# Attention and a residual MLP on one core: twelve products moved from GpSimd to VectorE, one turn moved by a step, and a bias added on VectorE in place of 48 matmuls

## The chip, the core and the metric

The kernel runs on one core of one Trainium2 chip. Five engines work side by side, each in the order of its own queue: TensorE (PE; its weight loads are listed as PEld), VectorE (DVE), ScalarE (ACT), GpSimd (POOL) and SyncE (SP), which only issues DMAs. Semaphores tie the queues together. The metric is the device time of one execution in microseconds; the time of a kernel is the median over its runs.

## What is computed

Attention with 16 query heads and 4 key/value heads over 8 batches of 384 positions, and behind it a mixer: a product over tokens and a two-layer product over channels, each with an affine map ahead of it and a residual sum. In the reference:

```python
scores = scale * np.matmul(q, k.transpose(0, 1, 3, 2))
attn = exp(scores - max) / sum
x = np.matmul(attn, v)                    # to (8, 384, 1024)

a1 = alpha1 * x + beta1
tok = np.einsum('ts,bsd->btd', w_tok, a1)
u = x + lam * tok
a2 = alpha2 * u + beta2
ch = np.maximum(a2 @ w_ch1, 0.0) @ w_ch2  # 1024 -> 4096 -> 1024
return u + lam * ch
```

Inputs and output are float32; matmuls run in bf16 with float32 sums.

## The kernel before

**Pairs and products.** The batches are worked in four pairs. Each pair has a *first product* (with w_ch1, to 4096 channels) and a *second product* (with w_ch2, back to 1024), and both are written as seven products over blocks in place of eight; `o` (1 to 7) numbers them. `pair(i)` is a generator that yields between small portions of matmuls, called steps below. In the first pair it delegates to `first_product` (matmuls at L681) and `second_product` (L752); in the other three the matmuls stand at L831 and L897.

**The side work.** Attention, the token product and what feeds the next pair are done by `side(b)`, one call for each batch. While pair `i` is in its second product, the side work of batches 2i+2 and 2i+3 runs between its steps; batches 0 and 1 come ahead of everything. For each of eight column pieces `p` of 128 columns there are the scores (L260) with the exponential on ScalarE (L269), the product with v (`av`, L295), the division by the sum (L300 a reciprocal, L303), then a1, then the *token product* (`tok`, L324), on VectorE the residual sum (L331) and alpha2 (L334), and at last the *turn*: the piece is transposed so that the next pair can take it as an operand, by DMA (L337) or, for batches 0 and 3 and the last pieces of odd batches, by TensorE (`turn`, L398) with a copy on ScalarE (L400). Scores, `av`, token products and turns of batches 2 and up take their PSUM from three banks in rotation (`three()`).

**lam and alpha1, beta1.** lam is multiplied into alpha1 and beta1 once, so the token product comes out scaled. For batches 0 to 3 (`fold`) only alpha1 is applied on VectorE (L309), and beta1 enters in the token product: behind the nine matmuls of L324, three at a time, there stand three more (L328) that multiply two small matrices, R (row sums of w_tok) and H (lam x beta1). For batches 4 to 7 beta1 is added on VectorE: L312 writes alpha1 x to float32, L313 adds beta1 and writes bf16. The vector for this, `h1`, has lam x beta1 on all 128 partitions and shares its memory with R and H (`folded`). It is filled by `rows4_on` (two memsets on POOL, two row loads on SP), `to_all` (two shuffles on VectorE, L1037) and `scale_beta` (two products on VectorE, L1040); before the change they run in the second pair's first product.

**Results.** The second product leaves float32 blocks of 128x512 in `hT`. `scaled` multiplies each with lam (L790) and stores it with a DMA from POOL's queue that adds to the output (L442). `flush` runs one waiting `scaled` at certain steps. In the first pair the L790 stands on POOL, in the others on VectorE. In the next pair's first product ScalarE copies partial sums into the same memory (L836), so these copies wait for the stores' landing. In the last 12 steps of `second_product` six such results are flushed, and three more in the next pair's first product.

**Weights.** The w_ch1 chunks are loaded by DMAs on POOL's queue (L183); VectorE makes the block sums of them (L510, L515), for which it waits for the load. L448 to L450 and L850 on VectorE make block sums of the turned pieces. L499 and L603 on VectorE make block sums of w_ch2 and of the hidden values, L767 adds partial results of the second product, L764 and L744 on ScalarE copy such results out of PSUM and back. In the first product of the first pair L693 to L722 on VectorE evacuate PSUM and L561, L565 make block sums.

**Order.** All engines run in an order written by hand (`manual_schedule`): the order in which the program calls the operations is the order of each queue. `put(ps, phase, at, f, ...)` places a call at step `at` of pair `ps`, in its first (0) or second (1) product; `side(b)` gives its own table of steps (0 to 42), which is shifted by 38 for the second batch of a pair. So an operation placed a step later can fall behind another one on each queue that both use.

Of the kernel before, what the change touches and what calls it, by code (L numbers as in the profile page):

```python
# [13 lines left out]
def kernel(  # L14
# [21 lines left out]
    nc = tc.nc  # L36
# [4 lines left out]
    MUL = mybir.AluOpType.mult  # L41
# [43 lines left out]
    g1, h1, al2, lam_t = (vecs[:, i] for i in range(4))  # L85
# [10 lines left out]
    turn, a2_turn = [0], [0]  # L96
# [117 lines left out]
    def side(b):  # L214
        vb = vt[b % 2]
        ess, avs, a1s, a2s, xr = {}, {}, {}, {}, {}
        first, fold = b < 2, b < 4
        kT_, qT_ = kTs.get(b, kT), qTs.get(b, qT)

        def x_of(p):  # L220
# [170 lines left out]
        def by_pe(p):  # L391
            return b in (0, 3) or b % 2 and p >= NP - (4 if first else 3)
# [14 lines left out]
        def put(k, *m):  # L407
            at.setdefault(k, []).append(m)
# [3 lines left out]
        for p in range(NP):  # L412
            put((4, 10, 14, 18, 24, 29, 33, 35)[p], av, p)
            put((8, 15, 17, 22, 27, 32, 36, 38 if b % 2 else 39)[p], tok_flip, p)
            if by_pe(p):
                put(((13, 20, 22, 28, 34, 37, 40, 42) if b == 3 else (0, 0, 0, 0, 0, 36, 39, 41))[p], turn, p)
        return at

    def loads(b):
# [21 lines left out]
    def store(b, ms, dw, o):  # L441
        nc.gpsimd.dma_start(out=by_tok(out[b])[:, ms, dw * 512:(dw + 1) * 512], in_=o, accum_op=ADD)  # L442
# [19 lines left out]
    def spare(i):  # L462
        at = 24 * S + i % 3 * 1024
        return hTf[:, at:at + 1024]
# [102 lines left out]
    def free_blocks(side, gp):  # L567
        for kind in (side + "1", side + "2"):
            if (kind, gp) in block_slot:
                free(block_slot.pop((kind, gp)))  # L570
# [201 lines left out]
    def pair(i):  # L772
        b0 = 2 * i
        lead = i == 0
# [12 lines left out]

        def scaled(o, b, ms, dw, t):
            if o != 2 or not last:
                (nc.gpsimd if lead else nc.vector).tensor_tensor(out=t, in0=t, in1=lam_t[:, dw * 512:(dw + 1) * 512], op=MUL)  # L790
            store(b, ms, dw, t)

        def flush(n=9):
# [18 lines left out]
        if lead:  # L812
            yield from first_product(flush)
            share_banks("sc0", "acc", "sc1", "sc2")
            yield from second_product(pairs["acc"], later, flush, scaled)
            return

        for g in range(NH // 2):
            X, Y, snap = {}, {}, {}
            for k, (o, e) in enumerate(SEQ1):  # L820
                t = 2 * g + e
# [54 lines left out]
        for k, o in enumerate(PLACE2):  # L876
            whole = not last and o != 4
            tail = last and o == 4
            for h in range(1 if whole else 2):
                for ms in range(NST - (tail and not h)):  # L880
# [37 lines left out]
                    if (whole or h == 1) and not (last and o == 4):  # L918
                        if o in (1, 6, 5):
                            q = ((1, 6, 5).index(o) * NST + ms) * 512  # L920
                            snap[o, ms] = snaps[:, q:q + 512]
                        else:
                            bb, dw = where[o]
                            t = snap[1, ms] if o == 7 else spare(ms).bitcast(f32)
                        for c0, c1, x in X[ms]:
                            if o == 1:
                                nc.scalar.copy(out=snap[o, ms], in_=x)
                            elif o in (6, 5):
                                tt(out=snap[o, ms], in0=x, in1=snap[1 if last or o == 6 else 6, ms], op=ADD)
                            elif o == 2 and last:  # L930
                                tt(out=t, in0=x, in1=lam_t[:, :512], op=MUL)
                            else:
                                base = {2: 1, 3: 1 if last else 5, 7: 5, 4: 6}[o]
                                tt(out=t[:, c0:c1], in0=x, in1=snap[base, ms][:, c0:c1], op=ADD)
                            if o == 7 and not last:
                                tt(out=snap[6, ms], in0=x, in1=snap[6, ms], op=ADD)
                        if o not in (1, 6, 5):
                            later.append((scaled, o, b0 + bb, ms, dw, t))
# [8 lines left out]
    with tc.manual_schedule(engines=order):  # L947
# [123 lines left out]
        def put(ps, phase, at, *m):  # L1071
            plan.setdefault((ps, phase, at), []).append(m)
# [17 lines left out]
        put(0, 0, 8, rows4_on, (3, 0), (3, 1))  # L1090
        put(0, 0, 30, to_all, 3, 0, 0)
        put(0, 0, 34, to_all, 3, 1, 1)
        put(1, 0, 20, rows4_on, (1, 0), (1, 1))
        put(1, 0, 54, to_all, 1, 0, 0)
        put(1, 0, 68, to_all, 1, 1, 1)
        put(1, 0, 62, scale_beta, 0)
        put(1, 0, 76, scale_beta, 1)
        for c in range(4):
            put(0, 0, (50, 72, 74, 44)[c], load_w2, "11", c)
            put(0, 0, (6, 14, 42, 46)[c], cast_w2, "21", c)  # L1100
# [11 lines left out]
        for ps in range(NB - 1):  # L1112
            c = 2 * ps + 2
            for i in range(9):
                put(ps, 0, (4, 8, 12, 16, 20, 24, 54, 58, 62)[i] if ps == 0 else 4 + 7 * i, load_next, c, 1)
                put(ps, 0, 70 + 3 * i if ps == 0 else 91 + 2 * i, load_next, c + 1, 1)
            put_flips(ps, 0, c, (44, 46, 50, 54, 58) if ps == 0 else range(76, 86, 2))
            put_all(ps, 1, side(c))
            for u, f, h in zip((8, 14, 14, 27, 32, 33) if ps == 0 else (10, 17, 18, 28, 33, 33),
                               (flip_q, flip_k, flip_q, flip_q, flip_k, flip_q), (0, 0, 2, 4, 2, 6)):  # L1120
                put(ps, 1, u, f, c + 1, h, 2)
            put_all(ps, 1, side(c + 1), lambda u: u + 38)
            for j, u in ((0, 77), (2, 80), (3, 83)) if ps == 0 else ((0, 76), (2, 79), (3, 81)):
                put(ps, 1, u, sums_a, j, 1 if j else 2)

        def steps(ps):
            done = [0, 0]
            for second in pair(ps):
                for f, *a in plan.pop((ps, second, done[second]), []):
                    f(*a)  # L1130
                done[second] += 1
                yield
            for key in [k for k in plan if k[0] == ps]:
                for f, *a in plan.pop(key):
                    f(*a)

        first = steps(0)
# [76 lines left out]
```

## Time and profile before

| what | value |
|---|---|
| median of 3 runs | 732.6 us (731.02, 732.6, 734.45) |
| profiled execution, its own time | 731.92 us |
| its span in the trace | 729.9 us |
| TensorE clock granted | 1.00 throughout |
| first product of the first pair (L681), last part | up to 128 us |
| second product of the first pair (L752) | 128 to 234 us |
| first product of the second pair (L831) | 234 to 309 us |
| VectorE busy, 200 to 250 us | 42.8 of 50 us |
| TensorE busy, 200 to 250 us | 48.2 of 50 us |

Times in the trace count from the start of the span. A row such as "PE MATMUL C<-w,arena 128*128 128x512" gives engine, operation, what is written and read by the program's names, and the sizes. Neighbouring matmuls overlap, so what one costs is read from the distance of starts, not from the row's length. In brackets stands how long the engine had been idle and what it waited for. The engines' busy shares and the rows around the change are shown in the prediction.

### The profile page before, as it was taken

The numbers are of one execution on the slowest core, as the hardware profiler recorded it, in microseconds if no ns is written. First come the engines' busy times: TensorE is split into PE (matmuls) and PEld (weight loads), VectorE is DVE, ScalarE is ACT, GpSimd is POOL, SyncE is SP. The second block draws the span as 40 slices with busy tenths as digits, with TensorE's granted clock in tenths as the row PEclk, the third lists the DMA queues.
The fourth block names the chain that finished last, engine by engine and source line by source line (L and its number), as shares of the span: only waits on it lengthen the run. The fifth ranks groups of instructions, "written<-read, shape, count | busy, mean of one in ns | idle before, by whom it ended". The sixth has DMA issues, their size and how long they took to land.

```text
span 729.9 us, 14511 instructions
## 1 busy us (share of the span) xinstructions
PE 717.4 (98%) x5716; PEld 408.7 (56%) x5716; DVE 543.9 (75%) x1009; ACT 373.8 (51%) x566; POOL 199.2 (27%) x242
## 2 busy tenths in 40 slices
PE   8899999999999999999999999999999999999998
PEld 4665555555555666555555566655555566654444
DVE  7888876577888988649678888748868988763354
ACT  7877666544563666643433466663333366650000
POOL 8844233221046551201022344200002222000011
PEclk9999999999999999999999999999999999999999
DMA  9999999999999999969989999998989999937965
GB/s 164 180 239 231 190 195 227 226 242 235 366 312 232 179 182 196 234 221 207 272 193 220 160 162 194 212 227 201 270 233 183 210 126 146 165 123 264 302 174 104
DMA packets 197616, 153.26 MB, mean 210 GB/s; under 512 B 90540, under 2 KB 175892, under 8 KB 197292
## 3 DMA queue, kind: packets, MB, share of 16 engines
q0 software_dynamic: 109872, 64.47, 65.4%
q1 hardware_dynamic: 86988, 87.42, 42.8%
q8 instruction: 44, 0.72, 0.4%
q10 hardware_dynamic: 688, 0.46, 0.2%
q14 instruction: 24, 0.20, 0.1%
HBM read 155.23 MB, written 39.85 MB: 267 GB/s over the span
## 4 chain that ended last, share of the span: by engine, by line
PE 90%; DVE 4%; POOL 2%; DMA 1%; issue 1%; ACT 1%; DVEq 0%; ACTq 0%; POOLq 0%
PE C L897 30%; PE X L831 17%; PE C L752 10%; PE Y L831 9%; PE Z L831 4%; PE sc L260 4%; PE X L681 4%; PE sc L295 3%; PE sc L324 3%; PE Y L681 3%; DMA ops<-obuf 1%; DVE pad L565 1%; PE Z L681 1%; PE tok L324 1%; POOL obuf L334 0%
## 5 line engine op out<-in xcount | busy, mean ns | idle before, releaser
L897 PE MATMUL C<-w,arena 128*128 128x512 bf16 (+2 forms) x744 | 168.3, 372 | 0.0
L269 ACT ACTIVATE es<-sc 128x1024 bf16<-128x1024 f32 x108 | 104.1, 1024 | 116.0 <-PE sc L260 107.6
L897 PEld LDWEIGHTS <-arena 128*128 128x128 bf16 x1040 | 94.8, 98 | 100.5 <-issue 5.1
L442 POOL DMA_DIRECT2D out_dram<-hT x45 | 40.0, 888 | 294.7 <-DVE hT L790 135.9
L836 ACT ACTIVATE hT<-X,bias 128x384 f32<-128x384 f32 x144 | 83.6, 582 | 60.0 <-PE X L831 55.2
L831 PEld LDWEIGHTS <-w 128*128 128x128 bf16 x768 | 75.1, 98 | 50.0
L831 PEld LDWEIGHTS <-pad 128*128 128x128 bf16 x576 | 56.4, 98 | 37.2
L183 POOL DMA_DIRECT2D w<-in_moe_w_ch_dram x48 | 45.4, 1002 | 105.6 <-PE X L831 36.5
L831 PE MATMUL X<-ops,w 128*128 128x384 bf16 x384 | 70.3, 326 | 0.0
L831 PE MATMUL X<-ops,pad 128*128 128x384 bf16 x384 | 70.3, 326 | 0.0
L897 PE MATMUL C<-pad,arena 128*128 128x512 bf16 (+2 forms) x296 | 70.2, 373 | 0.0
L324 PEld LDWEIGHTS <-wtokT 128*128 128x128 bf16 x576 | 39.0, 98 | 16.4 <-issue 3.4
L752 PEld LDWEIGHTS <-arena 128*128 128x128 bf16 x336 | 29.8, 98 | 30.0 <-issue 2.5
L331 DVE TENSOR_TENSOR xr<-sc,xr 128x384 f32<-128x384 f32 x48 | 26.5, 553 | 25.6 <-PE sc L324 14.3
L752 PE MATMUL C<-w,arena 128*128 128x512 bf16 x168 | 41.2, 379 | 0.0
L838 DVE TENSOR_TENSOR arena<-Y,hT 128x384 bf16<-128x384 f32 x48 | 26.5, 556 | 17.7 <-ACT hT L836 16.0
L295 PEld LDWEIGHTS <-es 128*128 128x128 bf16 x864 | 32.8, 97 | 11.3
L831 PE MATMUL Y<-ops,w 128*128 128x384 bf16 x192 | 39.1, 326 | 0.0
L831 PE MATMUL Z<-ops,w 128*128 128x384 bf16 x192 | 39.0, 326 | 0.0
L269 ACT ACTIVATE hT<-sc 128x1024 bf16<-128x1024 f32 x36 | 35.8, 1031 | 4.3 <-PE sc L260 4.0
L260 PE MATMUL sc<-qT,kT 64*128 64x384 bf16 (+2 forms) x504 | 37.2, 271 | 0.5 <-ACT hT L269 0.2
L842 ACT ACTIVATE arena<-X,bias 128x384 bf16<-128x384 f32 x48 | 27.9, 582 | 17.7 <-PE X L831 16.1
(190 smaller groups left out, 1175.1 us busy)
## 6 DMA issues: line engine op xcount, KB each, us to landing
w<-w2s SPq DMA_DIRECT2D x67, 512.0 KB, 5.1
w<-in_moe_w_ch_dram POOLq DMA_DIRECT2D x65, 512.0 KB, 9.8
pad<-w2s SPq DMA_DIRECT2D x25, 512.0 KB, 6.9
out_dram<-hT POOLq DMA_DIRECT2D x45, 256.0 KB, 7.1
out_dram<-xr SPq DMA_DIRECT2D x48, 192.0 KB, 5.3
q_raw<-in_q_dram POOLq DMA_DIRECT2D x28, 192.0 KB, 9.5
w2s<-w SPq DMA_DIRECT2D x10, 512.0 KB, 7.6
arena<-in_moe_w_ch_dram POOLq DMA_DIRECT2D x8, 512.0 KB, 15.9
```

The source lines that it names most:

```text
L183: nc.gpsimd.dma_start(out=w1[:, w1_slots[c]], in_=w1src[:, :, c * CW * P:(c + 1) * CW * P])
L260: nc.tensor.matmul(out=sc[:, hh, k % 4:k % 4 + n], lhsT=kT_[r, 2 * p // G, BLK[hh][sk], :], rhs=qT_[r, p, st:st + n, :], start=True, stop= ...
L269: nc.scalar.activation(out=e, in_=sc, func=EXP, scale=scale_qk)
L295: nc.tensor.matmul(out=av[:, hh, sq, :], lhsT=ess[k // 4][:, m % 2, k % 4, :], rhs=vb[:, sk, hk, :], start=(sk == 0), stop=(sk == NST - 1))
L324: nc.tensor.matmul(out=ps[:, tt, :], lhsT=wtokT[:, st, tt * P:(tt + 1) * P], rhs=a1s[p][:, st, :], start=(st == 0), stop=(st == NST - 1 an ...
L442: nc.gpsimd.dma_start(out=by_tok(out[b])[:, ms, dw * 512:(dw + 1) * 512], in_=o, accum_op=ADD)
L681: nc.tensor.matmul(out=ps[:, :n], lhsT=tb[G, o][:, dt, e * P:(e + 1) * P], rhs=opb(FIRST1[o], n)[:, dt], start=(o in (1, 2, 7) and dt == 0 ...
L752: nc.tensor.matmul(out=x, lhsT=lead_hid[:, t, FIRST2[o], ms * P:(ms + 1) * P], rhs=rhs[:, t % 4 * 512:(t % 4 + 1) * 512], start=(o in (1, ...
L831: nc.tensor.matmul(out=ps, lhsT=tb[g, o][:, dt, e * P:(e + 1) * P], rhs=opb(LEFT1[o])[:, dt], start=(o in (1, 2, 7) and dt == 0), stop=(dt ...
L836: nc.scalar.activation(out=snap[o, e], in_=ps, func=IDENT, bias=hi if o == 5 else lo)
L842: nc.scalar.activation(out=hid[:, t, 4], in_=ps, func=RELU, bias=hi)
L897: nc.tensor.matmul(out=x, lhsT=hid[:, t, LEFT2[o], ms * P:(ms + 1) * P], rhs=rhs[:, t % 4 * 512 + c0:t % 4 * 512 + c1], start=((not last o ...
```

## The change

Four edits, in the order of the diff:

- `fold` now holds for batches 0 and 1 alone. Batches 2 and 3 lose the three L328 matmuls in each of their 16 token products (48 in all); L309 becomes L312 and L313.
- Batch 3's turn of piece 2 moves from step 22 to step 23 of its table. At step 22 stands also the token product of piece 3, which was called after the turn and is now called before it.
- `scaled` uses VectorE in the first pair too: 12 L790 leave POOL's queue for VectorE's (nine in the second product, three in the next pair's first product). Their stores stay on POOL's queue.
- `h1` is filled in the first product of the first pair: row loads at step 40, shuffles at steps 54 and 64, scalings at 59 and 69. They leave the second pair's first product.

```diff
     def side(b):
         vb = vt[b % 2]
         ess, avs, a1s, a2s, xr = {}, {}, {}, {}, {}
-        first, fold = b < 2, b < 4
+        first = fold = b < 2
...
             if by_pe(p):
-                put(((13, 20, 22, 28, 34, 37, 40, 42) if b == 3 else (0, 0, 0, 0, 0, 36, 39, 41))[p], turn, p)
+                put(((13, 20, 23, 28, 34, 37, 40, 42) if b == 3 else (0, 0, 0, 0, 0, 36, 39, 41))[p], turn, p)
...
         def scaled(o, b, ms, dw, t):
             if o != 2 or not last:
-                (nc.gpsimd if lead else nc.vector).tensor_tensor(out=t, in0=t, in1=lam_t[:, dw * 512:(dw + 1) * 512], op=MUL)
+                nc.vector.tensor_tensor(out=t, in0=t, in1=lam_t[:, dw * 512:(dw + 1) * 512], op=MUL)
             store(b, ms, dw, t)
...
-        put(1, 0, 20, rows4_on, (1, 0), (1, 1))
-        put(1, 0, 54, to_all, 1, 0, 0)
-        put(1, 0, 68, to_all, 1, 1, 1)
-        put(1, 0, 62, scale_beta, 0)
-        put(1, 0, 76, scale_beta, 1)
+        put(0, 0, 40, rows4_on, (1, 0), (1, 1))
+        for i in range(2):
+            put(0, 0, 54 + 10 * i, to_all, 1, i, i)
+            put(0, 0, 59 + 10 * i, scale_beta, i)
```

The order of VectorE's queue around the last token products of the first pair is, in the changed program (new rows marked with +; p counts batch 3's pieces):

```
L331 L334 (p5)  L767  L499
L300 L303 L312 +L313 (p6)  +L790
L300 L303 L312 +L313 (p7)  +L790
L331 L334 (p6)  +L790
L331 L334 (p7)  L515  L448 L449 L450  +L790
```

## The prediction

> **What bounds the kernel now.** I read the page's busy shares first, then who TensorE waited for, then every engine in order of time in the second product of the first pair (127 to 234 us) and in the start of the second pair, since the change lies there. The page:
>
> ```profile
> PE 717.4 (98%) x5716; PEld 408.7 (56%) x5716; DVE 543.9 (75%) x1009; ACT 373.8 (51%) x566; POOL 199.2 (27%) x242
> ```
>
> TensorE sets the end: of 729.9 us it is idle 12.5. So what is removed from its queue counts in full unless a wait takes its place. The waits of TensorE in the window 126 to 236 us (engine, line, waited for, us in total, times, longest):
>
> ```profile
> PE sc L324 <- DVE a L309: 0.9, 1, 0.9
> PE sc L324 <- ACT es L269: 0.6, 1, 0.6
> PE sc L398 <- ACT es L269: 0.2, 1, 0.2
> ```
>
> There are three, 1.8 us together. TensorE's rows in order of time (start, length, row) show both prices, one token product's matmuls and the longest of these waits:
>
> ```profile
> 217.85 0.33 PE L324 MATMUL sc<-a,wtokT 128*128 128x128 bf16 x3
> 218.02 0.22 PE L328 MATMUL sc<-vecs 128*128 128x128 bf16 x1
> 218.07 0.33 PE L324 MATMUL sc<-a,wtokT 128*128 128x128 bf16 x3
> ...
> 222.78 1.03 PE L752 MATMUL C<-w,arena 128*128 128x512 bf16 x4
> 224.76 0.34 PE L324 MATMUL sc<-a,wtokT 128*128 128x128 bf16 x3 [0.95 <-DVE a L309]
> ```
>
> From 217.85 to 218.07 four matmuls start, so one costs 0.056 us, though its row is 0.22 long (they overlap). The group at 222.78 takes 0.87 (next starts in unbroken stretches), so the row at 224.76 could have begun at 223.65: 1.11 us lost. VectorE was late because of these rows (VectorE in order of time; then the two forms of L790, min/median/max ns):
>
> ```profile
> 220.26 0.69 DVE L767 TENSOR_TENSOR hT<-C,hT 128x512 f32<-128x512 f32 x1 [0.39 <-ACT hT L764]
> 220.87 2.02 DVE L499 TENSOR_TENSOR w<-w,pad 128x2048 bf16<-128x2048 bf16 x1
> ...
> 223.62 1.08 DVE L309 TENSOR_TENSOR a<-xr,vecs 128x384 bf16<-128x384 f32 x1
> ```
> ```profile
> L790 DVE TENSOR_TENSOR hT<-hT,vecs x30: 679/684/693, 328.6 to 716.4; 128x512 f32<-128x512 f32 x30
> L790 POOL TENSOR_TENSOR hT<-hT,vecs x12: 1263/1559/2112, 142.8 to 263.6; 128x512 f32<-128x512 f32 x12
> ```
>
> L499 takes 1.22 elsewhere and L309 0.557: both are stretched exactly while POOL runs an L790.
>
> **The change, part by part.** *48 matmuls (L328) gone*: 48 x 0.0567 = 2.72 us, all on TensorE in the second product, whose rows abut there.
>
> A page differs: the Trainium skill, "TensorE: Matmul & The Clock Gate", section "Back-to-back issue gap", gives about 81 ns for a sustained 128-column matmul with its weight load, which would make 48 x 0.081 = 3.9 us and my sum 1.2 us lower. The trace's 0.056 contradicts it and decides.
>
> *The turn of piece 2 of batch 3 behind a token product.* The 0.59 us wait at 204.89 is a token product that wants a PSUM bank whose exponential ends at 204.80, because the turn at 203.97 took the bank before it. In the new order the product takes the bank that was free, and the turn, 0.5 + 0.87 later, the one freed at 204.80. I count -0.59 (bounds -0.59 and 0). The 0.2 wait stays (bounds -0.24 and 0).
>
> *Products with lam (12 x L790) to VectorE, and one addition more (16 x L313, 0.557 us).* VectorE gets 12 x 0.684 + 16 x 0.557 = 17.1 us more, 9 of the 12 in this product, and loses the stretching (L334 1.77 for 0.56, L499 2.02 for 1.22, two L309 1.08 and 1.74 for 0.56). What decides is where a token product waits. I lay VectorE's new order end to end from the end of batch 3's token product 5 (218.69), by start distances in the rows (L331 to L334 0.59, L334 0.48, L499 1.13, L300 0.23, L303 and L312 0.59, L767 and L790 0.60, last L313 0.56): L767 starts at 1.57 (it waits for ScalarE, as now), L499 2.18, L300 3.31, L303 3.54, L312 4.13, L313 4.72 to 5.28. Token product 6 could start at 4.96, so it waits about 0.38 where it waited 1.11: -0.73 (bounds -1.11 and +0.2). Product 7 waits 0.07 more. The earlier ones have 0.6 to 4 us between L309's end and the product, against 0.59 for the addition: nothing counted.
>
> *beta1's two shuffles and two scalings to the first product (90 to 110 us).* There VectorE idles 2.1 us in each group of 14 steps, which hides the work. But the first shuffle (0.62 of queue) stands before L702, which ends its first half at 101.13, and TensorE overwrites that bank at 101.40: 0.62 - 0.27 = 0.35 lost; the second scaling does it again one group on. +0.7 (bounds 0 and 4 x 0.65 = 2.6, all of it on the path). Where they leave, in the second pair, TensorE never waited: 0. The two memsets (0.6 each) on POOL and two row loads on SP go ahead of weight loads and flips with POOL idle 5.1 us at 77.9: 0, or 1.2 if a load is late.
>
> *The last product with lam, and who waits for it.* POOL took its six late L790 whenever data was there; VectorE takes them at their place in the order. POOL's rows, before:
>
> ```profile
> 225.19 1.56 POOL L790 TENSOR_TENSOR hT<-hT,vecs 128x512 f32<-128x512 f32 x1
> 227.05 0.87 POOL L442 DMA_DIRECT2D out_dram<-hT  x1 [0.30 <-POOL hT L790]
> 232.10 0.92 POOL L183 DMA_DIRECT2D w<-in_moe_w_ch_dram  x1 [4.17 <-PE sc L398]
> ```
>
> In the new order the sixth stands behind the additions L448 to L450. Going on with the same ledger: L790 5.20, L300 5.80, L303, L312, L313 to 7.77, L790 7.69, L331 and L334 8.29, L790 9.36, L331 and L334 9.96, L515 11.03, L448 to L450 11.64, last L790 13.17 to 13.85, its store 0.3 later: 14.16. Call T the end of token product 7, 228.17 before and 8.50 in the ledger. The last store went at T-1.1 and goes at T+5.7; the w1 load that stands behind it on POOL's queue went at T+3.9 and goes at T+6.6. Both are awaited early in the second pair:
>
> ```profile
> 237.23 1.18 ACT L836 ACTIVATE hT<-X,bias 128x384 f32<-128x384 f32 x2 [0.72 <-PE X L831]
> ```
> ```profile
> 238.07 0.69 DVE L515 TENSOR_TENSOR pad<-w 128x1024 bf16<-128x1024 bf16 x1 [2.92 <-DMA w<-in_moe_w_ch_dram]
> 238.68 0.95 DVE L850 TENSOR_TENSOR ops<-ops 128x1536 bf16<-128x1536 bf16 x1
> ```
> ```profile
> 238.28 1.46 PE L831 MATMUL X<-ops,pad 128*128 128x384 bf16 x8
> ...
> 240.23 1.46 PE L831 MATMUL X<-ops,w 128*128 128x384 bf16 x8
> ```
>
> The copy at 237.23 writes where the last store reads, so it must wait for its landing; TensorE's group at 238.28 (T+10.1) overwrites the bank that the copy empties. All stores landed like this (us, min/median/max):
>
> ```profile
> DMA to landing us min/median/max: 3.9/7.1/13.5
> ```
>
> The last took 7.5, with more stores crowded before it than now; between 3.9 and 7.5 I take 5.5. Then T+5.7+5.5, the copy 0.6 and 0.1 of signals: T+11.9, 1.8 late. The load landed in 5.9: T+12.5, L515 0.6, L850 0.95: T+14.0, and the group at 240.23 (T+12.1), which reads what L850 writes, is 2.0 late. One wait covers the other: +2.0 (bounds 0, and 9.7 with a store of 13.5).
>
> A rule speaks against the change here: the Trainium skill, "SBUF — State Buffer", section "SBUF: two separate sides", says that VectorE and GpSimd share a port pair under an exclusive lock, and that GpSimd cannot write the descriptors of its own DMAs while VectorE holds it. The stretched rows above agree with the lock. By the rule the last store might be held up by one L790 more, 0.68 us by its row, and my sum would be 731.3; no row here shows a store held so.
>
> **Sum.** -2.72 - 0.59 - 0.73 + 0.07 + 0.7 + 2.0 = -1.3. The profiled execution took 731.92 (span 729.9 and 2.0 around it): 730.6. The median of the three runs shown is 0.7 above that execution, so 731.3 on its scale.
>
> **The rivals.** *The handover is hidden (faster).* Store and load land in time: stores of 3.9 are in the trace, and with POOL's L790 gone the queue is emptier. Against it: the load goes 2.7 later and had 0.6 of room. Without the 2.0: -3.3, 729.3 on the median's scale; with the front's 0.7 hidden too, 728.6; with all bounds good (-2.72 - 0.59 - 0.24 - 1.11), -4.7, 727.9.
>
> *The last store's landing becomes the bound (slower).* Its place is the copy at 237.23. With 13.5 us it lands at T+19.2 and TensorE stands 9.8 us: -3.3 + 9.8 = +6.5, 739.1. Slower by over 0.5% needs a wait of 7 us, a landing of 10.7. For: stores at 256 and 265 took 13.5 and 12.2. Against: these stood behind fresh w1 loads, and here the loads follow the store.
>
> *The change does nothing for TensorE's end.* VectorE idles only 2.0 us between 205 and 229; if every token product of batch 3 waits for the addition (0.59 x 8 = 4.7, for the 0.45 counted), the gain is eaten: -1.3 + 4.3 = +3.0, 735.6. For: the wait at 224.76. Against: the ledger keeps VectorE up with only 0.45 of waits.
>
> **How the numbers follow.** Chances: forecast 0.50, handover hidden 0.24, store late 0.16, VectorE late 0.10. A difference under 0.5% (3.7 us) is about what a measurement of this kernel cannot tell from no change. The hidden handover, with the front or a bound in its favour, is faster by more than that, nearly on the edge; with the forecast's own lower edge I give faster 0.24. Slower 0.17 from the late store and a part of the late VectorE; the rest, 0.59, is the same. The predicted time is the forecast's, 731.3; its own range is 729.5 to 733.5. The range is 727.9 (all bounds good) to 736.3 (a wait of 7 us).
>
> **What would show it.** Right: no L328 rows after 60 us; token products three matmuls apart at 0.17 and not 0.225; the wait at 204.89 gone, the one on L313 under 0.5; L499 back at 1.2; TensorE idle about 2 us within 8 us of the start of the second pair, released by ScalarE's L836 or VectorE's L850, after a POOL store issued within 1 us of the end of L752; two waits of 0.3 near 101 and 111. Wrong: the second pair starts without a gap (then near 729), or the gap is over 5 us, or waits on L313 recur at each token product.

## The result and the profile after

The changed kernel takes 738.01 us (median of 6 runs, 735.63 to 740.46), the kernel before 732.85 on the same chip (6 runs, 731.02 to 734.45). The ratio is 1.0065 with a 95% interval of 1.004 to 1.0091: slower by 0.65%, where 731.3 was forecast. The profiled execution took 736.76 (span 735.0), 4.84 more than the one before. The ratios here and below leave disturbed runs out and the medians don't, so the two need not agree to the last digit.

The busy shares of the changed kernel's page answer to the first line that the prediction shows:

```profile
PE 713.1 (97%) x5610; PEld 405.9 (55%) x5668; DVE 550.8 (75%) x1037; ACT 373.7 (51%) x566; POOL 181.0 (25%) x230
```

The span is 5.1 us longer though 48 matmuls are gone: TensorE idles more. (Its busy times can't be compared to the digit: its weight loads, PEld, are 48 fewer, its matmul records 106 fewer, so some are missing from this trace.) Where it idles is read from the start of each stage's first matmul. In the kernel before, the first pair's first product takes 69.23 us (58.84 to 128.07), its second 106.31 (to 234.38), the second pair's first product 72.80 (to 307.18). In the changed kernel these are 70.05, 103.41 and 80.52: +0.82, -2.90, +7.72. The stages behind them differ by 0.2 in all, the part ahead of them is 0.8 shorter. So the second product gained as meant, and the handover to the second pair lost it nearly three times over. The waits of TensorE in the changed kernel, 126 to 250 us:

```profile
PE X L831 <- DVE ops L850: 5.6, 1, 5.6
PE sc L324 <- DVE a L313: 0.7, 1, 0.7
PE sc L260 <- DVE xr L303: 0.3, 1, 0.3
PE sc L398 <- ACT es L269: 0.2, 1, 0.2
PE X L831 <- ACT hT L836: 0.2, 1, 0.2
PE C L752 <- issue: 0.2, 1, 0.2
```

The 5.6 is one wait. TensorE's rows around it, then VectorE's and GpSimd's, in order of time:

```profile
235.99 1.46 PE L831 MATMUL X<-ops,pad 128*128 128x384 bf16 x8 [0.23 <-ACT hT L836]
237.29 0.81 PE L831 MATMUL Z<-ops,w 128*128 128x384 bf16 x4
243.69 2.74 PE L831 MATMUL X<-ops,w 128*128 128x384 bf16 x8 [5.59 <-DVE ops L850]
246.23 0.98 PE L831 MATMUL Z<-ops,w 128*128 128x384 bf16 x4
```
```profile
233.62 0.68 DVE L515 TENSOR_TENSOR pad<-w,pad 128x1024 bf16<-128x1024 bf16 x1
242.08 0.69 DVE L515 TENSOR_TENSOR pad<-w 128x1024 bf16<-128x1024 bf16 x1 [7.77 <-DMA w<-in_moe_w_ch_dram]
242.69 0.95 DVE L850 TENSOR_TENSOR ops<-ops 128x1536 bf16<-128x1536 bf16 x1
```
```profile
230.93 0.84 POOL L442 DMA_DIRECT2D out_dram<-hT  x1 [2.95 <-DVE hT L790]
231.50 2.98 POOL L183 DMA_DIRECT2D w<-in_moe_w_ch_dram  x3
```

Read from the last fence up: the last store of the first pair goes at 230.93, because its product with lam (L790) now runs on VectorE behind the additions L448 to L450; the load of w1 stands behind it on GpSimd's queue and goes 0.57 later. The load lands at 242.05. VectorE has stood at L515 for it since 234.30, with L850 behind L515, which does not need the load at all; and TensorE stands for L850. The load alone, from its issue at 231.50 to its landing:

```profile
DMA to landing us min/median/max: 10.6/10.6/10.6
```

In the kernel before it was 5.9. Two windows (engines' busy times; the third number from the right is the granted clock, the last two are the DMA share and GB/s), first before, then after:

```profile
238.00:244.00 6.00, 6.00 (x39) 3.61 (x38) 5.70 (x11) 3.47 (x6) 2.01 (x3) 1.00 1.42 183
244.00:248.00 4.00, 4.00 (x26) 2.41 (x25) 3.86 (x4) 3.04 (x5) 3.70 (x6) 1.00 1.29 167
```
```profile
238.00:244.00 6.00, 0.41 (x3) 0.14 (x3) 1.92 (x3) 0.07 (x1) 0.00 (x0) 0.93 1.40 185
244.00:248.00 4.00, 4.00 (x18) 2.09 (x17) 2.98 (x7) 1.89 (x3) 1.27 (x2) 0.68 0.49 60
```

Behind the idle stretch the clock falls to 0.68 for a while. By starts (the next row stands at 247.05), the eight matmuls at 243.69 take 2.54 and the four behind them 0.82; before it was 1.30 and 0.65 (rows at 240.23, 241.53 and 242.18). That is 1.4 us more, so 5.6 + 0.2 + 1.4 = 7.2 of the 7.72.

### The profile page after: what moved, and what is told of

The parts are those of the page before. It is cut to its first block, busy times and chain, and to the rows that moved or that the text cites. A ratio compares the mean times of both kernels' runs of the same rounds, so it can differ in the third digit from the quotient of the medians.

```text
span 735.0 us, 14353 instructions
## 1 busy us (share of the span) xinstructions
PE 713.1 (97%) x5610; PEld 405.9 (55%) x5668; DVE 550.8 (75%) x1037; ACT 373.7 (51%) x566; POOL 181.0 (25%) x230
## 4 chain that ended last, share of the span: by engine, by line
PE 83%; DVE 8%; DMA 3%; POOL 2%; issue 2%; ACT 1%; SPq 0%; DVEq 0%; POOLq 0%; ACTq 0%
PE C L897 28%; PE X L831 17%; PE Y L831 8%; PE C L752 6%; PE sc L260 4%; PE Z L831 4%; PE X L681 3%; PE sc L295 3%; PE sc L324 3%; PE Y L681 2%; DMA w<-in_moe_w_ch_dram 1%; DMA w2s<-arena 1%; PE E L613 1%; PE tok L324 1%; PE av L295 1%
## 5 line engine op out<-in xcount | busy, mean ns | idle before, releaser
L897 PE MATMUL C<-w,arena 128*128 128x512 bf16 (+2 forms) x711 | 163.7, 372 | 1.6 <-issue 0.3
L269 ACT ACTIVATE es<-sc 128x1024 bf16<-128x1024 f32 x108 | 104.1, 1024 | 115.9 <-PE sc L260 107.6
L836 ACT ACTIVATE hT<-X,bias 128x384 f32<-128x384 f32 x144 | 83.6, 581 | 60.6 <-PE X L831 54.0
L324 PEld LDWEIGHTS <-wtokT 128*128 128x128 bf16 x576 | 37.4, 98 | 16.5 <-issue 3.2
L269 ACT ACTIVATE hT<-sc 128x1024 bf16<-128x1024 f32 x36 | 35.8, 1031 | 4.2 <-PE sc L260 4.0
```

The lines of the kernel that those rows point to most:

```text
L269: nc.scalar.activation(out=e, in_=sc, func=EXP, scale=scale_qk)
L324: nc.tensor.matmul(out=ps[:, tt, :], lhsT=wtokT[:, st, tt * P:(tt + 1) * P], rhs=a1s[p][:, st, :], start=(st == 0), stop=(st == NST - 1 an ...
L836: nc.scalar.activation(out=snap[o, e], in_=ps, func=IDENT, bias=hi if o == 5 else lo)
L897: nc.tensor.matmul(out=x, lhsT=hid[:, t, LEFT2[o], ms * P:(ms + 1) * P], rhs=rhs[:, t % 4 * 512 + c0:t % 4 * 512 + c1], start=((not last o ...
```

## The experiments

All runs at a glance. "First", "second" and "next" are the lengths of the first pair's first and second product and of the second pair's first product, by the starts of their first matmuls, in one profile each; "wait" is TensorE's longest in "next"; "behind" is how long after the last store of the first pair the awaited load was issued, "landed" what that load then took. Each ratio is to runs of the kernel before on the same chip, which for the rows below the second had medians of 732.75 to 733.37.

| kernel | median us (runs) | ratio to before, 95% | first | second | next | wait | behind | landed |
|---|---|---|---|---|---|---|---|---|
| before | 732.85 (6) | | 69.23 | 106.31 | 72.80 | none | 5.05 | 5.9 |
| the change | 738.01 (6) | 1.0065, 1.004 to 1.0091 | 70.05 | 103.41 | 80.52 | 5.6 L850 | 0.57 | 10.6 |
| lam_on_pool | 739.0 (4) | 1.0101, 1.0045 to 1.0157 | 69.98 | 112.03 | 72.80 | none | 9.39 | 5.9 |
| lam_only | 736.63 (6) | 1.0074, 1.0031 to 1.0117 | 69.30 | 105.19 | 79.30 | 3.7 L850 | 0.57 | 9.1 |
| last_on_pool | 734.77 (10) | 1.0026, 1.0003 to 1.0049 | 70.00 | 104.01 | 75.38 | 2.0 L850 | 0.59 | 9.1 |
| turn_only | 733.27 (10) | 1.0014, 0.9987 to 1.004 | 69.30 | 107.20 | 72.94 | none | 5.04 | 6.6 |
| flush_early | 733.7 (10) | 1.0018, 0.999 to 1.0047 | 70.04 | 105.28 | 74.42 | 1.4 L850 | 3.76 | 8.0 |
| sums_later | 734.44 (10) | 1.0007, 0.9991 to 1.0024 | 70.00 | 102.93 | 75.19 | 0.7 L836 | 0.57 | 7.9 |
| gap_loads | 736.86 (10) | 1.0043, 1.0005 to 1.008 | 70.00 | 104.01 | 80.97 | 5.2 L850 | 0.56 | 10.7 |
| early_and_later | 731.83 (10) | 0.9988, 0.9968 to 1.0008 | 70.04 | 104.65 | 74.15 | 0.9 L844 | 3.75 | 7.8 |
| best_late | 733.85 (12) | 0.9999, 0.9967 to 1.0032 | 69.27 | 104.16 | 77.26 | 2.4 L844 | 0.57 | 9.8 |
| best_early | 733.18 (12) | 0.9993, 0.996 to 1.0025 | 69.23 | 105.74 | 73.41 | 0.3 L844 | 3.76 | 7.7 |
| after_again | 738.24 (1) | | 69.99 | 105.14 | 79.71 | 4.6 L850 | 0.57 | 9.5 |
| no_stores | 730.96 (8) | 0.9979, 0.9932 to 1.0027 | 69.98 | 103.31 | 73.74 | 0.6 L844 | no store | 5.7 |

Five of these profiles run the same second product (the change, sums_later, gap_loads, best_late, after_again): 102.93 to 105.14, mean 103.9. A difference of under 2 us between two single profiles of this stage says little, therefore; the "first" column repeats to 0.1.

**The parts of the change.** First the parts were taken apart.

*lam_on_pool*: the change without its L790 edit.

```diff
-                nc.vector.tensor_tensor(out=t, in0=t, in1=lam_t[:, dw * 512:(dw + 1) * 512], op=MUL)
+                (nc.gpsimd if lead else nc.vector).tensor_tensor(out=t, in0=t, in1=lam_t[:, dw * 512:(dw + 1) * 512], op=MUL)
```

> The changed kernel with the first pair's twelve L790 back on POOL; the other three edits stay. Theory (the late last L790 on VectorE delays its store, and the weight loads behind it on POOL's queue, and TensorE waits for L850 at the start of the second pair): that wait of 5.6 us is gone, the second pair's first product is 72.8 long again in place of 80.5; the second product of the first pair is 104 to 105 (106.3 before, 103.4 changed), since POOL's L790 stretch VectorE's rows again and the additions stay; the first product of the first pair stays 0.8 longer than before. Total about 731 to 732. Rival (the removed matmuls bring the second pair forward, or the moved beta1 rows shift the loads, and the handover is late for that): the wait at L850 stays over 3 us and the total is 735 or more.

The wait at the handover was gone, as the theory had it, but the total missed it: the kernel was no faster than the changed one, because the second product took 112.03, where 104 to 105 was expected. VectorE's and TensorE's rows show why:

```profile
223.04 2.62 DVE L499 TENSOR_TENSOR w<-w,pad 128x2048 bf16<-128x2048 bf16 x1
227.50 2.43 DVE L313 TENSOR_TENSOR a<-a1f,vecs 128x384 bf16<-128x384 f32 x1
```
```profile
229.99 1.14 PE L324 MATMUL sc<-a,wtokT 128*128 128x128 bf16 x9 [4.30 <-DVE a L313]
```

L499 takes 1.22 and L313 0.56 in the changed kernel; here GpSimd works on an L790 of 1.55 to 1.57 us beside them (at 223.01 and 225.47, and at 227.95). One addition more per piece, stretched like that, makes the token product wait 4.3 us, and from 228 to 234 the granted clock is 0.50. The two parts of the change belong together: the additions fit only because the products with lam have left GpSimd.

*lam_only*: the kernel before with L790 on VectorE, and nothing else of the change.

> The kernel before with one edit: the first pair's L790 on VectorE. Theory: the wait at L850 appears here too, 4 to 8 us in the second pair's first product; the second product gains about 1 us as VectorE is no longer stretched. Total 736 to 740. Rival (the late handover needs the additions L313 or the moved beta1 too): under 1 us of wait and 732 to 733.

As the theory had it, but for a wait just under its 4 to 8: this one edit brings the loss (+6.50 in "next"). Its second product is 1.12 shorter, as expected, but that is within the scatter of single profiles, so what the moved products add to the 2.90 of the change is not shown. Of the 6.50 only 3.7 are the wait; the clock stays down longer here:

```profile
238.00:244.00 6.00, 2.32 (x10) 0.99 (x9) 3.17 (x6) 0.72 (x3) 0.00 (x0) 0.75 1.40 184
244.00:248.00 4.00, 4.00 (x14) 1.92 (x13) 2.36 (x5) 1.84 (x3) 2.12 (x3) 0.52 0.77 88
```

*last_on_pool*: the change, with the last of the six late L790 (`(o, ms) == (7, NST - 1)`) back on GpSimd.

> The changed kernel with only one of the twelve L790 on POOL: the last one of the second product (o 7, third token tile), the one behind the additions L448 to L450. Theory: its store goes about 3 us earlier relative to the last token product, the weight loads go when their slots are free and not behind the store, and the wait at L850 falls from 5.6 to under 1.5 us; total 730 to 732. Rival (the loads are slow for another reason than the store ahead of them): the wait stays over 4 us and the total is 735 or more.

It fell between the two. The last store went 2.95 ahead of the second pair's first matmul (0.60 in the change), but the load still followed it by 0.59 and landed in 9.1; the wait shrank to 2.0 and the clock stayed at 1.00. So bringing the store forward is not enough: the load was issued 2.36 ahead of the second pair, nearly as early as before the change (2.28), and still landed late.

*turn_only*: the kernel before with the turn at 23.

> The kernel before with one edit: the turn of piece 2 of batch 3 a step later. Theory: the 0.59 us wait of a token product for the exponential near 205 us is gone and nothing takes its place: 0.6 us faster, 732.2 where the kernel before has 732.8, all of it in the second product of the first pair. Rival (the turn then waits, or VectorE's late L309 takes the gain): 0.

The wait of 0.59 went and the one on L309 was longer, 1.68 for 0.95, as the rival said; the second product took 107.20 for 106.31, a difference within the scatter. VectorE, then TensorE, which waits for the L309 at 223.87:

```profile
220.52 2.63 DVE L499 TENSOR_TENSOR w<-w,pad 128x2048 bf16<-128x2048 bf16 x1
223.87 1.08 DVE L309 TENSOR_TENSOR a<-xr,vecs 128x384 bf16<-128x384 f32 x1
```
```profile
225.01 0.34 PE L324 MATMUL sc<-a,wtokT 128*128 128x128 bf16 x3 [1.68 <-DVE a L309]
```

**The handover.** Then each link of its chain was tried: the time of the last store, the order on VectorE, the loads behind the first, and the stores themselves.

*flush_early*: the late results are let go one turn sooner.

```diff
-                    if t % 8 == 3 and later and (later[0][1] == 1 or k > 16 and later[0][1] != 4):
+                    if t % 8 == 3 and later and (later[0][1] == 1 or k > 15 and later[0][1] != 4):
```

> The changed kernel with the six products with lam and their stores let go one turn of the second product sooner (k > 15 in place of k > 16). Theory (the load of w1 is late because it stands directly behind the last store, and nothing else): the last store leaves some 5 us sooner, at about 226, the load when the matmuls free its slot, at about 229.3, and it lands 5.9 later as it did before the change, at 235.2; L515 and L850 (0.69 + 0.95) end at 236.8, ahead of the 238.1 at which TensorE needs them. The wait of 5.6 is gone and with it the slow matmuls behind it (1.4): 729 to 731.5. If the landing stays near 9, a wait of about 2 is left: 731 to 733. Rival (VectorE has no room a turn sooner): the products run into the normalisation of batch 3, a wait of 1 to 4 us on L313 or L309 appears in the second product: 732 to 736.

The load, 3.76 behind the last store, landed in 8.0, and the wait was 1.4: the second of the theory's two cases, with the rival's wait on L313 beside it (1.2 for 0.7). The total, 733.7, lies above that case's 731 to 733 and inside the rival's.

*sums_later*: transfers as in the change; on VectorE L850 (L851 here) goes ahead of the sum that needs the load, and the sums for group 1 come later.

```diff
-                if k == 3 and g == 0:
-                    tt(out=opb(6), in0=opb(4), in1=opb(5), op=SUB)
                 if k == 2 and g == 0:
                     sum_w1(0, 4)
-                if k in (2, 5, 8, 11) and g + 1 < NH // 2:
-                    sum_w1(g + 1, {2: 5, 5: 7, 8: 6, 11: 4}[k])
+                    tt(out=opb(6), in0=opb(4), in1=opb(5), op=SUB)
+                at = (5, 8, 9, 11) if g == 0 else (2, 5, 8, 11)
+                if k in at and g + 1 < NH // 2:
+                    sum_w1(g + 1, (5, 7, 6, 4)[at.index(k)])
```

> The changed kernel with L850 issued ahead of the first sum that needs the load (L515), and the sums for group 1 put later in group 0 (turns 5, 8, 9, 11 in place of 2, 5, 8, 11). Loads and stores stay as they are: the load still lands at about 242. Theory (it is the order on VectorE that turns the late landing into 5.6 us of an idle TensorE): the wait on L850 goes; the first products of group 1 that need the sum, at about 242, wait until some 243.4, 1.5 us or less; the clock does not dip. 730 to 732.5. Rival (the landing itself is what is paid for, wherever its reader stands: VectorE behind the load still holds up L838 and L840, and with them the banks of PSUM): the wait comes back at another line, 4 us or more: 735 to 738.

The waits of TensorE, 128 to 320 us:

```profile
PE X L831 <- ACT hT L836: 0.9, 2, 0.7
PE sc L324 <- DVE a L313: 0.7, 1, 0.7
PE Y L831 <- DVE arena L844: 0.6, 1, 0.6
```

L850 is gone from the list, and the waits left in "next" are 1.5 us in three pieces, at the last store's landing (L836) and at the sums behind the load (L844); by the starts the stage is still 2.4 longer than before. The load was issued 0.57 behind the store, and landed in 7.9, 2.0 later than before the change, yet VectorE reached L850 at 234.83, ahead of the landing at 240.03. So it is the order on VectorE that turns a late load into a standing TensorE: that link is shown, and the ratio (1.0007 for 1.0065) goes with it. The profile flatters this version, however: its run, 732.06, is the fastest of the ten, and the median of 734.44 lies above the theory's 730 to 732.5 and below the rival's 735.

*gap_loads*: the change, with four memsets on GpSimd between the first and the second of the three loads (its lines stand 5 further down, L855 for L850).

```diff
     def load_w1(c):
+        if c == order1[4] and not filled:
+            filled.append(c)
+            for _ in range(4):
+                nc.gpsimd.memset(filler, 0.0)
```

> The changed kernel with four memsets of a scratch tile on GpSimd (2 us or so) between the first and the second of the three loads at the handover. Theory A (the three loads, issued 0.9 us apart, share the DMA engines, and the first is slow because the others overtake it): the first lands 8.5 us or less after its issue in place of 10.6, the wait on L850 falls from 5.6 to 3.5 or less: 734.5 to 736. Theory B (what slows it is the store 0.6 us ahead of it and a busy VectorE, the loads behind it do nothing): it lands at 9.5 to 11 us as before, the wait stays at 5 to 6, and the later loads come 2 us later without anyone waiting: 737 to 739.

The second load went 3.2 behind the first in place of 0.9, and the first took 10.7: theory B, with a median of 736.86 for its 737 to 739. Holding the loads behind back by 2.3 us does not make the first faster. It does not clear them altogether: between the first load's issue and its landing GpSimd's queue moved 1.43 MB here (1.44 in the change, 0.77 in the kernel before, 0.63 in no_stores), where that load is 0.5 and the store ahead of it 0.3, so transfers issued behind it were moved before it was complete.

*no_stores*: the change without the six accumulating stores of (o = 6, 7) in the first pair; these parts of the output are left out (its L845 is L844 elsewhere).

```diff
-            store(b, ms, dw, t)
+            if not lead or o not in (6, 7):
+                store(b, ms, dw, t)
```

> The changed kernel without six accumulating stores (the (o = 6, 7) parts of the second product of batches 0 and 1, which are missing from the output); the six products with lam still run on VectorE. The load at the handover has no store ahead of it on GpSimd's queue and is issued when the matmuls free its slot, some 2 us ahead of the handover. Theory S (the stores ahead of it are what makes it land late): it lands 6 or less after its issue, the wait on L850 falls to 0 to 1, as before the change: 729 to 731.5. Theory R (the stores are not what matters; the landing is long because of the rest that runs there, VectorE's row of 0.35 to 0.7 us operations first of all): it still takes 8 or more, the wait is about 1.5 as in flush_early: 731 to 733.

GpSimd's row, the load's landing, and VectorE's row:

```profile
231.04 0.87 POOL L183 DMA_DIRECT2D w<-in_moe_w_ch_dram  x1 [16.92 <-PE sc L398]
```
```profile
DMA to landing us min/median/max: 5.7/5.7/5.7
```
```profile
236.72 0.69 DVE L515 TENSOR_TENSOR pad<-w 128x1024 bf16<-128x1024 bf16 x1 [0.61 <-DMA w<-in_moe_w_ch_dram]
```

Theory S: with VectorE as busy as in the change, the load lands in 5.7 once no store is ahead of it, and VectorE waits 0.61 for it in place of 7.77. The stores do both: they hold back the issue (2.30 ahead of the second pair's first matmul here, 0.03 in the change), and they lengthen the landing.

*after_again*: the changed kernel, profiled once more.

> The changed kernel as it is, profiled once more, for the scatter of the landing: the load directly behind the last store landed 10.6 after its issue in one profile, 10.7 in gap_loads and 7.9 in sums_later, whose transfers are issued in the same order. If the landing is a property of the order of issue, with a scatter of 2 to 3 us, it falls anywhere from 8 to 11 here, with a wait on L850 of 3 to 6; if it goes with the wait itself (TensorE standing still), it is 10 to 11 again.

9.5, with a wait of 4.6. So the landing has a scatter, as in the first of the two cases: six loads issued 0.6 behind the last store in kernels with all of the first pair's L790 on VectorE took 7.9 to 10.7 (the change, lam_only, sums_later, gap_loads, best_late, after_again).

**Versions that might beat both.** *early_and_later* has both edits of flush_early and sums_later.

> Both edits of flush_early and sums_later in the changed kernel. If the handover is all that the change lost, neither a wait on L850 nor one on L510 is left in the second pair's first product, the stage takes 72.8 again, and what is left is the change's gain in the second product (2.9) less its price in the first (0.8): 729.5 to 731, under the kernel before. If the sooner products make VectorE late for batch 3, as in flush_early's rival, 731 to 735.

The handover's loss fell to 1.35 (74.15), with the wait on L313 at 1.2 and one of 0.9 on L844. The median, 731.83, lies in the range that was given for products that make VectorE late, 731 to 735. The ratio, 0.9988, does not part it from the kernel before.

*best_late* is sums_later with the sums for group 1 still later, and with beta1's shuffles and scalings moved; *best_early* is the same with `k > 15`.

```diff
-                at = (5, 8, 9, 11) if g == 0 else (2, 5, 8, 11)
+                at = (8, 9, 10, 11) if g == 0 else (2, 5, 8, 11)
...
-            put(0, 0, 54 + 10 * i, to_all, 1, i, i)
-            put(0, 0, 59 + 10 * i, scale_beta, i)
+            put(0, 0, 64 + 14 * i, to_all, 1, i, i)
+            put(0, 0, 65 + 14 * i, scale_beta, i)
```

> sums_later with two further edits: the sums for group 1 at turns 8, 9, 10, 11 of group 0 (so that VectorE reaches the load some 2 us later and L838, L840 and L844 are ahead of it), and the two shuffles and scalings of beta1 put into VectorE's idle stretches of the first product (turns 64, 65, 78, 79 in place of 54, 59, 64, 69). Theory: the first product takes 69.3 again (70.05 in the changed kernel), the second keeps its 103, and the second pair's first product takes 72.8 to 73.7 (a wait of up to 0.9 on L836, for the last store's landing, is left): a gain of 2.5 to 3.4 on the kernel before: 729.5 to 731, faster by 0.3 to 0.5%. Rival (VectorE, with its work pushed behind the load, is late at group 1: a wait on L844 or L510 of 1 us or more): 731 to 733, no difference from before.

> best_late with the products with lam let go a turn sooner (k > 15). Theory: no wait on L836, the wait on L313 in the second product stays at 1.2 (104.65 in early_and_later): first product 69.3, second 104.65, second pair's first 72.8 to 73.3: 1.2 to 1.7 under the kernel before: 730.5 to 732. Rival: as in best_late.

The move of beta1 did what was expected of it: 69.27 and 69.23 in "first", as before the change. In best_late the rival's wait on L844 came: the sums were put too late for a load that took 9.8, and the total, 733.85, is above both ranges. VectorE (first row) then does four sums, L844 behind them, and TensorE (second) waits for it.

```profile
241.40 0.69 DVE L515 TENSOR_TENSOR pad<-w 128x1024 bf16<-128x1024 bf16 x1 [2.29 <-DMA w<-in_moe_w_ch_dram]
```
```profile
245.01 0.81 PE L831 MATMUL Y<-ops,w 128*128 128x384 bf16 x4 [2.37 <-DVE arena L844]
```

best_early came close to the 72.8 (73.41), but its second product took 105.74 for the 104.65 expected, with waits of 0.8 on L499, 0.7 on L303 and 1.2 on L313. No version is faster than the kernel before by more than its interval; those that mend the handover give the change's loss back, not more.

## Why the prediction was wrong, step by step

- *The 48 matmuls, -2.72*: right. By starts each of the 16 token products took 0.67 before and takes 0.50 now, 2.7 in all. The listed waits of the second product went from 1.7 to 1.4, so 106.31 - 2.72 - 0.3 = 103.3, and it took 103.41 (103.9 as a mean of five).
- *The turn, -0.59*: the wait on L269 went, as argued. Alone it brings no gain (turn_only); in the change a wait of 0.3 on L303 came up.
- *Token product 6*: by the starts it is 0.88 late (222.15 for 220.40 + 0.87) in place of the ledger's 0.38 (1.11 before), inside its bounds; product 7 loses 0.07, as forecast. The ledger of VectorE's new order held: the last store was forecast at T+5.7 and the load at T+6.6; T, the end of product 7's last row as in the prediction, is 225.32, which makes them T+5.6 and T+6.2.
- *beta1 in the first product, +0.7*: right in size (+0.7 to +0.8 in all nine profiles that have it at these steps) and in kind: two waits on L702 stand at 101.08 and 110.87, and the loss goes when the work moves into VectorE's idle stretches.
- *The handover, +2.0*: the place, the wait and the chain (store, load, L515, L850, the group that reads it) were right; the step that failed is "The load landed in 5.9". It took 10.6. With it, the same working gives T+6.6 + 10.6 + 0.6 + 0.95 = T+18.75, and 6.65 late for the 2.0. The rest is a term that was missing: TensorE, once it has stood for 5.6 us, comes back at a lower clock, 1.4 us. The sum would have been -1.3 + 4.65 + 1.4 = +4.75, 736.7 for the profiled execution's 736.76 (closer than the terms deserve, which is luck: the second product gained about 1 less, and the start of the execution was 0.8 shorter).
- *Why the range missed it*: the bounds of the +2.0 were worked from the store's scatter (3.9 to 13.5) and took the load's 5.9, one landing, as fixed. The two loads behind it in the same trace took 7.8 and 9.6; as a bound for a load that other transfers crowd, these were the nearest rows, and 9.6 would have given 5.7 late, 735.0 on the median's scale. Also, the range stopped at a wait of 7 us, 736.3, short of the 9.7 that the term itself was given, which makes 739.1; the handover lost 7.72, inside that bound, but by the load and the clock and not by the store.
- *The rivals*: the last store's landing became no bound; it took 4.3 (5.5 forecast), and its reader, the copy L836, cost 0.23. VectorE did not become late in the second product; in lam_on_pool, with the same additions beside GpSimd's L790, it did.
- *The rule on the shared port*: the store was not held up; it went at 230.93, 0.30 behind the end of L790 (229.95 + 0.68). The Trainium skill's "SBUF — State Buffer", section "SBUF: two separate sides", agrees with the runs in its other half, the exclusive lock: L313 takes 0.56 and, beside GpSimd's L790, 2.43.

## What to carry to other kernels

When work moves off a queue that also issues DMAs, follow that queue to its next load and price the load's landing as a range, from the most crowded landings in the trace, not from its own quiet one: a store issued just ahead of it changes it. Then look at what stands behind the load's reader on the engine that waits; an instruction there that does not need the load, as L850, can be put ahead of it: here that took the ratio from 1.0065 to 1.0007 with the load issued as late as in the change. And a stretch in which TensorE idles several us (3.7 and more here) costs more than its length.

## What the runs showed of the hardware that was not expected

- *At this handover, a load behind accumulating stores lands later, the more so the closer they are.* On GpSimd's queue, the same 512 KB load took 5.7 with no store ahead, 5.9, 6.6 and 5.9 when it was issued 5 to 9 us behind the last store, 7.7, 7.8 and 8.0 at 3.8 us, and 7.9 to 10.7 at 0.6 us. Closeness is not all: later in the same stage of the kernel before, loads issued 4.2 us behind a store took 10.6 and 11.9. What spreads the last group is open, too: the issues of sums_later (7.9) and gap_loads (10.7) have the same order and spacing ahead of the load. What the stores do to the load on its way is not shown.
- *The clock behind an idle stretch.* Waits of 3.7, 4.6 and 5.6 us (lam_only, after_again, the change) were followed by a granted clock of 0.52, 0.67 and 0.68 in the window 244 to 248; waits of 1.4, 2.0 and 2.4 (flush_early, last_on_pool, best_late) by 1.00. Two more fit in: 5.2 in gap_loads, then 0.62 in that window, and 4.3 in the second product of lam_on_pool, with 0.50 from 228 to 234. The stage's loss beyond the waits was 2.8 in lam_only. The Trainium skill, "TensorE: Matmul & The Clock Gate", section "Part 1: The HAM clock gate", says that the clock halves after an idle window of about 3.4 us and comes back after about as long a busy one; these eight agree with it on the fall; the way back is not even, since in lam_only 246 to 248 still has 0.53, though the matmuls came back at 242.45.
- *VectorE beside GpSimd.* L313 2.43 for 0.56 and L499 2.62 for 1.22 (lam_on_pool), L309 1.75 for 0.56 (turn_only, at 225.68), each while GpSimd runs an L790: the VectorE instruction is lengthened by 1.2 to 1.9 us, where the L790 itself takes 1.55 to 1.57.
